# A recurrent attention with an MLP behind it: whole 128-token tiles for the first four units, 64x64 tiles for the rest

## The chip, the cores and the metric

The kernel runs on one core of a Trainium2 chip. The metric is the time of one execution on the device, in microseconds (us). The engines are TensorE (PE in the profile, with its weight loads as PEld), VectorE (DVE), ScalarE (ACT), GpSimd (POOL) and SyncE (SP), which issues the DMAs. Each engine takes its instructions in order and waits for others on semaphores.

## The reference

```python
# r, k, v, w: (batch 4, heads 8, tokens 768, 48); u: (8, 48)
state = 0                                            # (4, 8, 48, 48)
for t in range(768):
    y[t]  = r[t] @ (state + (u * k[t]) outer v[t])
    state = w[t][:, None] * state + k[t] outer v[t]
x = y as (3072, 384)                                 # tokens by heads*48
h = x @ w_in                                         # (384, 2048)
g = where(h > 0, h, exp(min(h, 0)) - 1)
out = g @ w_out                                      # (2048, 384)
```

The decay w lies between 0.80 and 0.95. All inputs are float32.

## The kernel before

The 768 tokens are six chunks (c = 0 to 5) of 128 tokens by 4 batches, 512 columns of x each. The attention of a chunk is done in four *units* of 128 rows, 24 units in all. A unit is a *pair*: 64 tokens of two batches, so units 0 and 1 of a chunk hold its first 64 tokens (batches 0, 1 and 2, 3), units 2 and 3 its other 64. The 8 heads lie as 4 pairs of heads (`NP`), one in partitions 0 to 47, one in 64 to 111.

A unit's steps, with the planner's names: `es` and `gs` are two scans on VectorE that turn w into running products inside the 64 tokens; `rh` and `kh` multiply r and k by them; `rkc`, `pd`, `md` and `sp` form the diagonal (u times r times k) and spread it over a matrix `am` (on ScalarE for units 0 to 7, on GpSimd later); `s` (`score`) transposes k and multiplies k with r; `mk` copies the scores above the diagonal into `am`; `v` (`value`) multiplies `am` with v, and k transposed with v (the update of the state, `pu`); `state_part`, half in `score`, half in `value`, adds r times the state. `xh` and `xl` take the result out of PSUM as two rounded parts; `sc` and `up` scale the state and add the update. Units 0 and 1 have no state before them (`first`): they skip `sc` and `state_part`, and ScalarE copies their update.

All of these matmuls are float32 in pieces of the array. Scores, state parts and values use tiles of 64 rows by 32 columns (`job`, and the loop over `j in range(4)` in `score` and `value`), the transposes and the diagonal the whole width. On the chip each such matmul of the code shows as two records; a transpose shows as one.

The MLP of a chunk has 16 steps (`f`), each with `g1` (9 matmuls, x times w_in), four small steps on ScalarE and VectorE (`r1`, `r2`, `stt`, `gh`, `gl`), and `g2` (9 matmuls into `acc`). Its operands are float32r, split into a high and a low part. In chunks 0 and 1 the first six steps are done in two halves of 256 columns (`FH`): the first needs only the chunk's units 0 and 1. The weights come in as 64-bit floats; for each f, ScalarE and VectorE convert them during chunk 0 (`a`, `cand`, `cb`, `cc`, `wh`, `wl`).

The order is made by `Plan.order`: it plays all steps through with the costs in `COST`, the buffer counts in `SLOTS` and the due times that follow from `BEGINS`, and lets each engine take, of what is ready, the step that is due first. The code is then emitted in that order; each engine runs its own list. SP issues the loads of w, k (with r), rk, v and of the raw weights from one queue in this order, and waits in it for buffers to come free.

Of the kernel before, what the change touches and what calls it, by code (L numbers as in the profile page):

```python
# [40 lines left out]
def _pieces():  # L41
    res = []
    for h in range(H):
        s, e = h * D, (h + 1) * D
        while s < e:
# [10 lines left out]
COST = dict(es=1.2, gs=1.5, pc=0.2, pd=0.9, md=0.2, spa=2.0, rh=0.62, kh=0.62, rk=0.48, rku=0.48, prk=1.2, prku=1.35, dg=0.5, mk=0.65, up=0.48, sc=0.48, xl=0.48,  # L56
            cand=0.56, cv=0.96, wl=0.88, stt=0.62, gl=0.64, fl=1.35, kt=0.53, xh=0.48, a=0.92, wh=0.82, r1=0.6, r2=0.62, gh=0.62,
            sp=1.95, s=1.4, s0=1.1, s2=0.95, v=1.4, v0=1.2, v2=0.95, g=2.05, out=0.6)
# [8 lines left out]
COLS = 128  # L67
PAD = 160
# [4 lines left out]
SLOTS = dict(w=2, k=3, rk=2, v=4, eg=2, md=2, am=2, kt=2, pa=1, pb=1, wg=2, ph=2, m=2, gh=2, gl=2, x=2, acc=1, raw0=1, x0=1, x1=1, x1a=1, x1b=1)  # L73
# [134 lines left out]
def mlp(nc, w_h, w_l, ps_acc, ps_h, ml, gp, po, dst, last=False):  # L208
# [9 lines left out]

    def g1(s, x):
        f, lo, hi = s["f"], s["lo"], s["hi"]  # L220
        xh, xl = (z[:, :, lo:hi] for z in x)
        s["ph"] = ph = ps_h.tile([P, N], F32, tag="ph", name="ph")[:, 0:hi - lo]
        for k in range(NK):
            for n, (w, x_) in enumerate(((w_h, xh), (w_h, xl), (w_l, xh))):
                for z in range(0, P, COLS):
                    nc.tensor.matmul(ph[z:z + COLS], w[:, f, 0, k, z:z + COLS], x_[:, k, :],  # L226
                                     start=(k == n == 0), stop=(k == NK - 1 and n == 2))
# [19 lines left out]
    def g2(s):  # L247
        f, lo, hi = s["f"], s["lo"], s["hi"]
        for m in range(NK):
            parts = 2 if (f == NF - 1 and m == NK - 1 and last) else 1  # L250
            for q in range(parts):
                s_ = slice(q * (hi - lo) // parts, (q + 1) * (hi - lo) // parts)
                a_ = accs()[m][:, lo + s_.start:lo + s_.stop]
                for n, (w, g) in enumerate(((w_h, s["gh"]), (w_h, s["gl"]), (w_l, s["gh"]))):
                    for z in range(0, P, COLS):
                        nc.tensor.matmul(a_[z:z + COLS], w[:, f, 1, m, z:z + COLS], g[:, s_],  # L256
                                         start=(f == n == 0 and lo == 0), stop=(f == NF - 1 and q == parts - 1 and n == 2))
# [22 lines left out]
def rwkv_elu_kernel(ctx, tc, wkr, rk, vp, u, uz, gkrw, gv, gu, wraw, out):  # L280
# [28 lines left out]
    upper = kp.tile([P, L], F32, name="upper")  # L309
    upper4 = upper.bitcast(U32).unsqueeze(1).unsqueeze(1).broadcast_to([P, 2, NP, L])  # L310
# [4 lines left out]
    units = [dict(c=i // B, b=(2 * (i % STEP), 2 * (i % STEP) + 1), i=i, first=i < STEP, last=i >= NU - STEP) for i in range(NU)]  # L315
    spans = lambda x: x.rearrange("d (s t) -> d s t", s=NS)
    scan = lambda x, z: spans(x[:, z])
    raws, xts = {}, {}

    def constants():  # L320
        nc.scalar.preload_act_table_set("natural_log_exp_and_others")
        nc.vector.memset(reset, 2.0 ** -62)
        nc.vector.memset(scan(reset, 0)[:, :, L:L + 1], 1.0)
# [3 lines left out]
        nc.vector.memset(upper, 1.0)  # L327
        for z in range(2):
            rs = slice(L * z, L * z + L)
            nc.gpsimd.affine_select(out=ident_h[rs], in_=ident_h[rs], pattern=[[1, L]], compare_op=ALU.is_equal,  # L330
                                    fill=0.0, base=0, channel_multiplier=-1)
            nc.gpsimd.affine_select(out=upper[rs], in_=upper[rs], pattern=[[1, L]], compare_op=ALU.is_gt,
                                    fill=0.0, base=0, channel_multiplier=-1)
# [47 lines left out]

    def r_hat(u_):
        r = spans(u_["r"].rearrange("d p t -> d (p t)"))
        tt(r, r, scan(u_["eg"], 1)[:, :, 0:L], ALU.mult)  # L384

    def k_hat(u_):
        k = spans(u_["k"].rearrange("d p t -> d (p t)"))
        tt(k, k, scan(u_["eg"], 0)[:, :, 1:L + 1], ALU.mult)

    def flag(u_):  # L390
        junk = at.tile([R2, 2, CWS], BF16, tag="junk", name="junk", bufs=1)
        act(junk, u_["eg"], AF.Relu, bias=lim, accum_out=flags[:, u_["i"]:u_["i"] + 1])  # L392
# [25 lines left out]
    def spread_act(u_):  # L418
        u_["am"] = am = at.tile([P, 2, NP, L], F32, tag="am", name="am", bufs=SLOTS["am"])
        for q in range(2):  # L420
            for p in range(NP):
                act(am[:, q, p], ident_h, AF.Copy, scale=u_["md"][:, q, p:p + 1])  # L422
# [14 lines left out]
    def state_part(u_, swap):  # L437
        for n in range(2 * NP):
            for h in range(2):
                p, x = HEADS[h ^ swap][n]  # L440
                rs, e = slice(64 * (x // 2), 64 * (x // 2) + D), (16, 48, 0, 32)[x]
                job(u_, h, p, x, st[rs, u_["b"][h], p, e:e + 32], u_["r"][rs, p, L * h:L * h + L], start=(swap == 1 and n < 4), stop=False)

    def score(u_):
# [5 lines left out]
        u_["pa"] = pa = both[:, :, 0:NP * L].rearrange("t q (p s) -> t q p s", p=NP)  # L450
        u_["pu"] = both[0:R2, :, 0:NP * D].rearrange("d h (p e) -> d h p e", p=NP)
        u_["py"] = both[:, :, NP * L:NP * L + NK * L].rearrange("d h (k t) -> d h k t", k=NK)
        for p in range(NP):
            for j in range(4):
                js, ts = slice(32 * j, 32 * j + 32), slice(64 * (j // 2), 64 * (j // 2) + L)
                for q in range(2):
                    rs = slice(64 * q, 64 * q + D)
                    nc.tensor.matmul(pa[js, 1 - q, p], u_["k"][rs, p, js], u_["r"][rs, p, ts], start=True, stop=True)  # L458
        if not u_["first"]:
            state_part(u_, 1)  # L460

    def mask(u_):
        nc.vector.copy_predicated(u_["am"], upper4, u_["pa"])
# [5 lines left out]
    def scale_state(u_):  # L469
        b = slice(u_["b"][0], u_["b"][0] + 2)  # L470
        tt(sv[:, b], sv[:, b], u_["pc"].rearrange("d (p h) o -> d h p o", h=2).broadcast_to([R2, 2, NP, D]), ALU.mult)

    def value(u_):
        v, am, kt = u_["v"], u_["am"], u_.get("kt")
        rows = [slice(L * h, L * h + L) for h in range(2)]
        if not u_["first"]:
            state_part(u_, 0)
        for n, (p, x) in enumerate(VALUES):
            for h, rs in enumerate(rows):
                job(u_, h, p, x, v[rs, P * p + 32 * x:P * p + 32 * x + 32], am[rs, 1 - x // 2, p],  # L480
                    start=(u_["first"] and n < 4), stop=(u_["last"] and n >= len(VALUES) - 4))
        if u_["last"]:
            return
        for p in range(NP):
            for j in range(4):
                js = slice(32 * j, min(32 * j + 32, R2))
                for h, rs in enumerate(rows):
                    nc.tensor.matmul(u_["pu"][js, h, p], kt[rs, p, js], v[rs, P * p + 80 * (j // 2):P * p + 80 * (j // 2) + D],  # L488
                                     start=False, stop=(p == NP - 1))

    def columns(u_, t):
        lo = u_["i"] % B * C
        return t[:, :, lo:lo + C].rearrange("d k (h t) -> d h k t", h=2)

    def x_high(u_):
# [3 lines left out]
        nc.scalar.copy(columns(u_, xts[c][0]), u_["py"])  # L499

    def x_low(u_):
        xh, xl = (columns(u_, t) for t in xts[u_["c"]])
        tt(xl, u_["py"], xh.bitcast(F32), ALU.subtract)  # L503

    def update(u_):
        b = slice(u_["b"][0], u_["b"][0] + 2)
        if not u_["first"]:
# [54 lines left out]
    for u_ in units:  # L562
# [6 lines left out]
        add(("es", i), "DVE", K["es"], lambda u_=u_: e_scan(u_), [("const",), ("ld_w", i)], lock=True)  # L569
# [3 lines left out]
        if not u_["first"]:  # L573
# [19 lines left out]
        if not u_["first"]:  # L593
            add(("sc", i), "DVE", K["sc"], lambda u_=u_: scale_state(u_), [("pc", i), ("up", i - STEP)], lock=True)
# [209 lines left out]
```

## Time and profile before

| | |
|---|---|
| runs | 557.33, 560.1, 564.27 us (median 560.1) |
| profiled execution | 559.8 us, span 558.0 us |
| granted TensorE clock, mean | 0.942 |
| PE busy | 515.2 us (92%), 8009 records |
| DVE, ACT, POOL busy | 348.4 us, 284.1 us, 69.9 us |
| data moved | 47.91 MB, mean 86 GB/s |

"Busy" counts the time in which an engine runs at least one instruction; small matmuls overlap, so their own durations add up to more. A row of a group or of a timeline gives the line, engine and operation, the tile written and the tiles read, and in brackets how long the engine stood idle before it and what ended that; "issue" is idle time for which the profile shows no releaser. The instruction queue (q8) carries the program itself to the engines.

### The profile page before, as it was taken

To read this page: it belongs to the slowest core of one execution; us is meant where nothing else is said; L and a number is where in the kernel's file an instruction comes from. 1 tells how busy PE (TensorE), PEld (TensorE's weight loads), DVE (VectorE), ACT (ScalarE), POOL (GpSimd) and SP (SyncE) were. 2 spreads that over 40 slices of the span, in tenths; PEclk is the share of its full clock that TensorE was granted. 3 is DMA by queue.
4 is the path that set the end of the run, shared out by engine and by line. 5 is a ranking of instruction groups with operands and counts; after the bars stand their busy time and mean duration, and the time that the engine had idled before them with its cause. 6 is when DMAs were issued, how large, how long until landed. Compare 5 with 4: busy or idle time off the path is not lost.

```text
span 558.0 us, 17756 instructions
## 1 busy us (share of the span) xinstructions
PE 515.2 (92%) x8009; PEld 433.9 (78%) x8009; DVE 348.4 (62%) x524; ACT 284.1 (51%) x564; POOL 69.9 (13%) x75
## 2 busy tenths in 40 slices
PE   6478789998889999999999999999999999999993
PEld 6368788886778887888888888888887888788882
DVE  7489789997546786249684358883377763333331
ACT  5367378776535445266443455553464544544441
POOL 1000000000111513003430003530032110000000
PEclk8556899998798999999999999999999999999998
DMA  8833945111532331014420055231052000010001
GB/s 263 254 117 121 288 140 170 56 35 59 179 97 75 110 93 57 4 53 142 115 64 2 2 167 152 80 98 55 2 173 80 3 3 1 12 47 1 0 0 62
DMA packets 17298, 47.91 MB, mean 86 GB/s; under 512 B 2112, under 2 KB 2496, under 8 KB 17216
## 3 DMA queue, kind: packets, MB, share of 16 engines
q1 hardware_dynamic: 17072, 46.57, 27.2%
q8 instruction: 65, 1.06, 0.8%
q14 instruction: 17, 0.14, 0.1%
q10 hardware_dynamic: 144, 0.13, 0.1%
HBM read 41.98 MB, written 4.72 MB: 84 GB/s over the span
## 4 chain that ended last, share of the span: by engine, by line
PE 86%; DVE 5%; issue 4%; ACT 3%; DMA 1%; DVEq 0%; ACTq 0%
PE acc L256 36%; PE ph L226 35%; PE pa L435 6%; PE pa L458 3%; PE pa L488 3%; PE pb L448 2%; PE pb L412 1%; ACT am L422 1%; DVE w_l L542 1%; DVE wg L532 1%; DMA w<-in_wkr_dram 1%; DVE wg L536 0%; DVE k L384 0%; DVE eg L379 0%; ACT wg L524 0%
## 5 line engine op out<-in xcount | busy, mean ns | idle before, releaser
L237 DVE SCALAR_TENSOR_TENSOR m<-m,ph 128x512 f32<-128x512 f32 (+1 forms) x108 | 67.4, 625 | 112.9 <-ACT m L234 112.3
L231 ACT ACTIVATE m<-ph 128x512 f32<-128x512 f32 (+1 forms) x108 | 59.2, 548 | 139.2 <-PE ph L226 138.6
L226 PE MATMUL ph<-xh,w_h 128*128 128x512 f32 (+1 forms) x324 | 124.6, 384 | 5.0 <-ACT w_h L539 1.7
L256 PE MATMUL acc<-gh,w_h 128*128 128x512 f32 (+1 forms) x325 | 124.5, 383 | 0.7 <-ACT gh L241 0.7
L226 PE MATMUL ph<-xh,w_l 128*128 128x512 f32 (+1 forms) x324 | 122.5, 378 | 2.4 <-DVE w_l L542 2.0
L256 PE MATMUL acc<-gl,w_h 128*128 128x512 f32 (+1 forms) x325 | 121.0, 372 | 1.8 <-issue 1.5
L226 PE MATMUL ph<-xl,w_h 128*128 128x512 f32 (+1 forms) x324 | 122.2, 377 | 0.2 <-DVE xl L503 0.2
L256 PE MATMUL acc<-gh,w_l 128*128 128x512 f32 (+1 forms) x325 | 121.2, 373 | 0.0
L245 DVE TENSOR_TENSOR gl<-m,gh 128x512 fp32r<-128x512 f32 (+1 forms) x108 | 69.0, 642 | 32.7 <-ACT gh L241 31.9
L241 ACT CAST gh<-m 128x512 fp32r<-128x512 f32 (+1 forms) x108 | 61.3, 571 | 45.0 <-DVE m L237 37.3
L226 PEld LDWEIGHTS ph<-xh,w_h 128*128 128x128 f32 x324 | 64.6, 199 | 16.7 <-ACT w_h L539 2.1
L226 PEld LDWEIGHTS ph<-xh,w_l 128*128 128x128 f32 x324 | 64.5, 199 | 13.5 <-DVE w_l L542 2.9
L256 PEld LDWEIGHTS acc<-gh,w_h 128*128 128x128 f32 x325 | 63.1, 194 | 12.8 <-ACT gh L241 1.1
L226 PEld LDWEIGHTS ph<-xl,w_h 128*128 128x128 f32 x324 | 64.7, 200 | 10.2 <-DVE xl L503 0.7
L256 PEld LDWEIGHTS acc<-gl,w_h 128*128 128x128 f32 x325 | 63.2, 195 | 12.0 <-issue 1.8
L256 PEld LDWEIGHTS acc<-gh,w_l 128*128 128x128 f32 x325 | 63.1, 194 | 10.3
L234 ACT ACTIVATE m<-m 128x512 f32<-128x512 f32 (+1 forms) x108 | 63.2, 585 | 3.3
L428 POOL TENSOR_SCALAR_AFFINE_SELECT am<-md 64x512 f32<-64x512 f32 x32 | 27.7, 864 | 220.4 <-DVE md L402 176.6
L395 POOL TENSOR_TENSOR rk<-rk 128x384 f32<-128x384 f32 x16 | 18.7, 1170 | 155.2 <-DMA rk<-in_rk_dram 154.8
L392 ACT ACTIVATE junk<-eg,lim 112x1040 bf16<-112x1040 f32 x24 | 27.8, 1158 | 11.0 <-DVE eg L379 11.0
L379 DVE TENSOR_TENSOR_SCAN eg<-w,reset 112x520 f32<-112x520 f32 x24 | 31.3, 1303 | 0.8
L370 DVE TENSOR_TENSOR_SCAN eg<-w,reset 112x520 f32<-112x520 f32 x24 | 30.5, 1269 | 1.6 <-DMA w<-in_wkr_dram 1.5
(73 smaller groups left out, 500.1 us busy)
## 6 DMA issues: line engine op xcount, KB each, us to landing
k<-in_wkr_dram SPq DMA_DIRECT2D x24, 448.0 KB, 4.8
wrawx<-in_wraw_dram SPq DMA_DIRECT2D x10, 768.0 KB, 4.5
v<-in_vp_dram SPq DMA_DIRECT2D x24, 256.0 KB, 5.9
rk<-in_rk_dram SPq DMA_DIRECT2D x16, 384.0 KB, 4.2
w<-in_wkr_dram SPq DMA_DIRECT2D x24, 227.9 KB, 3.9
wraw<-in_wraw_dram SPq DMA_DIRECT2D x6, 768.0 KB, 5.3
out_dram<-o SPq DMA_DIRECT2D x17, 256.0 KB, 2.3
ub<-in_u_dram SPq DMA_DIRECT2D x1, 192.0 KB, 9.9
```

Of the source, the lines that this page charges most:

```text
L226: nc.tensor.matmul(ph[z:z + COLS], w[:, f, 0, k, z:z + COLS], x_[:, k, :], start=(k == n == 0), stop=(k == NK - 1 and n == 2))
L231: act(s["m"], s["ph"], AF.Relu, scale=-1.0)
L234: act(s["m"], s["m"], AF.Exp, scale=-1.0)
L237: stt_(s["m"], s["m"], -1.0, s["ph"], ALU.add, ALU.max)
L241: nc.scalar.copy(s["gh"], s["m"])
L245: nc.vector.tensor_tensor(s["gl"], s["m"], s["gh"].bitcast(F32), ALU.subtract)
L256: nc.tensor.matmul(a_[z:z + COLS], w[:, f, 1, m, z:z + COLS], g[:, s_], start=(f == n == 0 and lo == 0), stop=(f == NF - 1 and q == parts ...
L370: nc.vector.tensor_tensor_scan(out=eg[:, 0][:, ::-1], data0=u_["w"][:, 1:CWS + 1][:, ::-1], data1=reset[:, 0][:, ::-1], initial=0.0, op0=A ...
L379: nc.vector.tensor_tensor_scan(out=u_["eg"][:, 1], data0=u_["w"][:, 0:CWS], data1=reset[:, 1], initial=0.0, op0=ALU.mult, op1=ALU.max)
L392: act(junk, u_["eg"], AF.Relu, bias=lim, accum_out=flags[:, u_["i"]:u_["i"] + 1])
L428: nc.gpsimd.affine_select(out=am[rs].rearrange("t q p s -> t (q p) s"), in_=u_["md"][rs].rearrange("t q p -> t (q p)").unsqueeze(2).broadc ...
L435: nc.tensor.matmul(u_["py"][32 * j:32 * j + 32, h, k], l, r, **flags)
```

## The change

Units 0 to 3 are now one batch by 128 tokens each (`whole`); the 20 others stay pairs. For a whole unit scores are 8 matmuls of the code with 128x128 outputs, values 16 with 32 output rows and 128 columns, the update 8. The scans run over 128 tokens; their constants (`reset`) are rewritten on GpSimd ahead of unit 4. None of the four has a state before it, so none has `sc` or `state_part`, and ScalarE copies each update. The mask and the diagonal of a whole unit are 128x128 per head. In the pairs, scores and updates go by 64x64 tiles: 16 matmuls each in place of 32. The columns of chunk 0's x keep their place; its half steps read and write them through a two-part view (`cut`, `fold`). There are three v buffers in place of four, and some costs of the planner changed. What is fed in is laid out to match.

```diff
-            sp=1.95, s=1.4, s0=1.1, s2=0.95, v=1.4, v0=1.2, v2=0.95, g=2.05, out=0.6)
+            sp=1.95, s=1.55, s0=1.6, s2=1.05, v=1.7, v0=1.55, v2=1.2, g=2.05, out=0.6)
-SLOTS = dict(w=2, k=3, rk=2, v=4, eg=2, md=2, am=2, kt=2, pa=1, pb=1, wg=2, ph=2, m=2, gh=2, gl=2, x=2, acc=1, raw0=1, x0=1, x1=1, x1a=1, x1b=1)
+SLOTS = dict(w=2, k=3, rk=2, v=3, eg=2, md=2, am=2, kt=2, pa=1, pb=1, wg=2, ph=2, m=2, gh=2, gl=2, x=2, acc=1, raw0=1, x0=1, x1=1, x1a=1, x1b=1)
...
+    units = [dict(c=i // B, i=i, whole=i < B, last=i >= NU - STEP, L=C if i < B else L,
+                  b=slice(i, i + 1) if i < B else slice(2 * (i % STEP), 2 * (i % STEP) + 2)) for i in range(NU)]
...
     def spread_act(u_):
-                act(am[:, q, p], ident_h, AF.Copy, scale=u_["md"][:, q, p:p + 1])
+                act(am[:, q, p], ident if u_["whole"] else ident_h, AF.Copy, scale=u_["md"][:, q, p:p + 1])
...
     def score(u_):
         for p in range(NP):
-            for j in range(4):
-                js, ts = slice(32 * j, 32 * j + 32), slice(64 * (j // 2), 64 * (j // 2) + L)
+            for lo in range(0, C, u_["L"]):
                 for q in range(2):
-                    rs = slice(64 * q, 64 * q + D)
-                    nc.tensor.matmul(pa[js, 1 - q, p], u_["k"][rs, p, js], u_["r"][rs, p, ts], start=True, stop=True)
+                    rs, ts = slice(64 * q, 64 * q + D), slice(lo, lo + u_["L"])
+                    nc.tensor.matmul(pa[ts, 1 - q, p], u_["k"][rs, p, ts], u_["r"][rs, p, ts], start=True, stop=True)
...
     def value(u_):
-        rows = [slice(L * h, L * h + L) for h in range(2)]
+        rows = [slice(0, C)] if whole else [slice(L * h, L * h + L) for h in range(2)]
...
         for p in range(NP):
-            for j in range(4):
-                js = slice(32 * j, min(32 * j + 32, R2))
-                for h, rs in enumerate(rows):
-                    nc.tensor.matmul(u_["pu"][js, h, p], kt[rs, p, js], v[rs, P * p + 80 * (j // 2):P * p + 80 * (j // 2) + D],
-                                     start=False, stop=(p == NP - 1))
+            for h, rs in enumerate(rows):
+                for z in range(2):
+                    m = 64 - 16 * z
+                    nc.tensor.matmul(u_["pu"][64 * z:64 * z + m, h, p], kt[rs, p, 64 * z:64 * z + m], v[rs, P * p + 80 * z:P * p + 80 * z + D],
+                                     start=whole, stop=(whole or p == NP - 1))
...
+        again = i > 0 and units[i - 1]["whole"] != u_["whole"]
+        if again:
+            add(("reset", i), "POOL", 1.2, lambda u_=u_: set_reset(nc.gpsimd, u_), [("gs", i - 1)])
```

Three places in the instruction order. A row has the line, the operation, the tile written and the tiles read, the shape of the output, and how many follow each other. First TensorE at the program's start, before: transposes and scores of units 0 and 1 (`pb`, then `pa` and `acc`), values and the first update matmuls of unit 0.

```order
L448 MATMUL pb<-ident,k 128x112 x4
L458 MATMUL pa<-k 32x64 x32
L448 MATMUL pb<-ident,k 128x112 x4
L458 MATMUL acc<-k 32x64 x32
L435 MATMUL pa<-am,v 32x64 x32
L488 MATMUL pa<-v,kt 32x48 x6
L488 MATMUL pa<-v,kt 16x48 x2
```

The same place now:

```order
L460 MATMUL pb<-ident,k 128x112 x4
L468 MATMUL pa<-k 128x128 x8
L460 MATMUL pb<-ident,k 128x112 x4
L468 MATMUL acc<-k 128x128 x8
L447 MATMUL pa<-am,v 32x128 x16
L503 MATMUL pa<-v,kt 64x48
L503 MATMUL pa<-v,kt 48x48
```

The order of the steps is the same; 32 scores became 8, 32 values 16, and an update of 32 (four times the last two rows) became one of 8. Unit 1's value follows, now behind the diagonal of unit 2.

Second, TensorE at the closing stretch of a pair unit inside the MLP, before: an MLP matmul, then the second half of the state part, the values and the first update matmuls.

```order
L256 MATMUL acc<-gh,w_l 128x512
L435 MATMUL pa<-k,st 32x64 x16
L435 MATMUL pa<-am,v 32x64 x32
L488 MATMUL pa<-v,kt 32x48 x6
L488 MATMUL pa<-v,kt 16x48 x2
```

And now:

```order
L260 MATMUL acc<-gh,w_l 128x512
L447 MATMUL pa<-k,st 32x64 x16
L447 MATMUL pa<-am,v 32x64 x32
L503 MATMUL pa<-v,kt 64x48
L503 MATMUL pa<-v,kt 48x48
```

State part and values are as they were; the update that ends the stretch is 16 matmuls (eight times the last two rows) in place of 32.

Third, ScalarE at the program's start, before, from the first unit's diagonal (`md`, `am`) to the first state copy; `wg` and `w_h` are steps of a weight conversion.

```order
L416 COPY md<-pb 128x8
L422 ACTIVATE am<-ident_h,md 128x64 x8
L416 COPY md<-pb 128x8
L524 ACTIVATE wg<-wraw 128x768
L422 ACTIVATE am<-ident_h,md 128x64 x8
L467 COPY kt<-pb 128x448
L392 ACTIVATE junk,flags<-eg,lim 112x1040
L467 COPY kt<-pb 128x448
L524 ACTIVATE wg<-wrawx 128x768
L499 CAST xh<-pa 128x2x3x64
L539 CAST w_h<-wg 128x768
L510 COPY st<-pa 112x8x48
```

And now:

```order
L428 COPY md<-pb 128x8
L434 ACTIVATE am<-ident,md 128x128 x8
L428 COPY md<-pb 128x8
L434 ACTIVATE am<-ident,md 128x128 x8
L544 ACTIVATE wg<-wraw 128x768
L482 COPY kt<-pb 128x448
L404 ACTIVATE junk,flags<-eg,lim 112x2x516
L544 ACTIVATE wg<-wrawx 128x768
L482 COPY kt<-pb 128x448
L559 CAST w_h<-wg 128x768
L519 CAST xh<-pa 128x6x64
```

The first conversion step (`wg<-wraw`) moved behind unit 1's diagonal, and both diagonals are of 128 columns.

More of the change, by code (lines that the diff above doesn't have):

```diff
@@ L308, in rwkv_elu_kernel @@
     ident_h = kp.tile([P, L], F32, name="ident_h")
-    upper = kp.tile([P, L], F32, name="upper")
-    upper4 = upper.bitcast(U32).unsqueeze(1).unsqueeze(1).broadcast_to([P, 2, NP, L])
+    upper = kp.tile([P, C], F32, name="upper")
+    upper_h = kp.tile([P, L], F32, name="upper_h")
+    above = {n: t.bitcast(U32).unsqueeze(1).unsqueeze(1).broadcast_to([P, 2, NP, n]) for n, t in ((C, upper), (L, upper_h))}
     ub = cst.tile([P, DM], F32, name="ub")
@@ L480, in value @@
                 job(u_, h, p, x, v[rs, P * p + 32 * x:P * p + 32 * x + 32], am[rs, 1 - x // 2, p],
-                    start=(u_["first"] and n < 4), stop=(u_["last"] and n >= len(VALUES) - 4))
+                    start=(whole and n < 4), stop=((whole or u_["last"]) and n >= len(VALUES) - 4))
         if u_["last"]:
@@ L592, in rwkv_elu_kernel @@
         before = []
[L593 to L594 removed]
+        if not u_["whole"]:
+            add(("sc", i), "DVE", K["sc"], lambda u_=u_: scale_state(u_), [("pc", i)] + [("up", x["i"]) for x in units[max(0, i - B):i - 1] if set(range(4)[x["b"]]) & set(range(4)[u_["b"]])], lock=True)
             before.append(("sc", i))
[L596 to L597 removed]
+        add(("s", i), "PE", K["s0" if u_["whole"] else "s2" if u_["last"] else "s"], lambda u_=u_: score(u_), [("rh", i), ("kh", i), ("sp", i), ("const",)] + before)
+        add(("mk", i), "DVE", K["mk0" if u_["whole"] else "mk"], lambda u_=u_: mask(u_), [("s", i), ("sp", i)])
         if not u_["last"]:
@@ L602, in rwkv_elu_kernel @@
             after.append(("v", i - 1))
-        add(("v", i), "PE", K["v0" if u_["first"] else "v2" if u_["last"] else "v"], lambda u_=u_: value(u_), after,
+        add(("v", i), "PE", K["v0" if u_["whole"] else "v2" if u_["last"] else "v"], lambda u_=u_: value(u_), after,
             due=BEGINS[c] - (B - 1 - i % B) * STAG - 2.0 if c > 1 else None)
@@ L607, in rwkv_elu_kernel @@
         if not u_["last"]:
-            add(("up", i), FIRST if u_["first"] else "DVE", K["up"], lambda u_=u_: update(u_), [("xl" if u_["first"] else "xh", i)])
+            add(("up", i), FIRST if u_["whole"] else "DVE", K["up"], lambda u_=u_: update(u_), [("xl" if u_["whole"] else "xh", i)])
     for f in range(NF):
```

129 lines of the change are left out of this document (73 added, 56 removed).

## The prediction

> **What bounds the kernel now.** I read the page first (busy time, the chain that ended last), then a table by stage, then what TensorE waited for.
>
> ```profile
> span 558.0 us, 17756 instructions
> PE 515.2 (92%) x8009; PEld 433.9 (78%) x8009; DVE 348.4 (62%) x524; ACT 284.1 (51%) x564; POOL 69.9 (13%) x75
> ...
> PE 86%; DVE 5%; issue 4%; ACT 3%; DMA 1%; DVEq 0%; ACTq 0%
> ```
>
> TensorE is busy for 92% of the span and is 86% of the chain; the third name, "issue", is time in which the engine waited for nothing that the profile shows. The stages, with columns PE, weight load, VectorE, ScalarE, GpSimd (busy us and instructions), granted clock, DMA share, GB/s:
>
> ```profile
> 0.00:29.00 29.00, 16.97 (x435) 15.23 (x436) 18.09 (x30) 12.49 (x31) 2.72 (x11) 0.65 0.82 249
> 29.00:53.00 24.00, 20.31 (x86) 18.56 (x86) 21.92 (x33) 17.72 (x45) 0.00 (x0) 0.50 0.40 132
> 53.00:75.00 22.00, 15.67 (x574) 13.90 (x573) 17.00 (x29) 11.03 (x21) 0.00 (x0) 0.92 0.79 236
> 75.00:126.00 51.00, 50.88 (x368) 44.09 (x366) 48.43 (x74) 38.99 (x79) 0.00 (x0) 1.00 0.28 90
> 126.00:173.00 47.00, 39.58 (x1097) 35.80 (x1098) 25.36 (x44) 21.80 (x62) 5.50 (x6) 0.85 0.40 117
> 173.00:558.00 385.00, 371.75 (x5457) 306.27 (x5455) 217.56 (x318) 182.10 (x330) 61.67 (x58) 1.00 0.19 58
> ```
>
> Up to 75 us no engine is full, and VectorE, which converts the weights, is the busiest (57.0 of 75). From 75 to 126 TensorE has no gap. From 126 to 173 it loses 7.4 us to gaps and runs at a clock of 0.85. After that it loses 13 us in 385. So from 75 us on, whatever TensorE is spared comes off the end. Its waits from 75 us on (total, times, longest):
>
> ```profile
> PE pa L488 <- issue: 4.7, 3, 2.3
> PE pb L412 <- issue: 1.5, 1, 1.5
> PE acc L256 <- issue: 1.5, 1, 1.5
> PE ph L226 <- issue: 1.4, 2, 1.0
> ```
>
> That is 9.1 us without a visible cause, nearly all right behind small matmuls. The longest of all lies earlier. These are the DMA queues over the span (packets, MB, share), in 17.6 to 23.7 us, and in 23.7 to 26.3 us, and the matmul that ended that gap:
>
> ```profile
> q8 instruction: 65, 1.06, 0.8%
> ...
> q1 hardware_dynamic: 722, 1.88, 105.4%
> ...
> q8 instruction: 1, 0.02, 3.1%
> ...
> 26.31 0.47 PE L435 MATMUL acc<-am,v 64*32 64x64 f32 x16 [5.11 <-issue]
> ```
>
> Sixty-five packets of 16 KB feed 8009 matmuls and as many weight loads: one per some 123 pairs. While the data queue filled the DMA engines (105%) no such packet moved; one moved in the next 2.6 us, and TensorE went on. I read "issue" as waiting for its own program. A later gap gives the pace:
>
> ```profile
> 425.32 0.45 PE L435 MATMUL pa<-k,st 48*32 48x64 f32 x32
> ...
> 426.28 0.62 PE L488 MATMUL pa<-v,kt 64*32 64x48 f32 x42
> 427.87 0.34 PE L488 MATMUL pa<-v,kt 64*16 64x48 f32 x19 [0.97 <-issue]
> ```
>
> A stretch of state, value and update matmuls began at 425.32, had run off its 32 state, 64 value and 42 of its update records at 426.90 (some 140 of 160), and got more at 427.87, 2.55 us after it began.
>
> **The change part by part.** The sum is made against the profiled execution: 559.8 us (span 558.0), beside a median of 560.1 over runs from 557.33 to 564.27.
>
> *Program supply.* An f32 matmul of the code is two records here (32 state matmuls of the code in the two halves of a unit are 64). A pair unit ran 64 score, 64 state, 64 value and 64 update records; now scores and updates are 32 each. The closing stretch is 32+64+32 = 128. Behind it come MLP matmuls: nine between 263.38 and 265.65 in the rows below, 0.25 us each. In the 2.55 us that a packet took, the new stretch uses 128 records (about 1.6 us) and some four matmuls: 132, under the 140 that were at hand. So most of the 9.1 us goes; I take 7.5, ends 0 and 9. The Trainium skill, "Runtime: NRT & Kernel Launch", section "Instruction fetch mechanics", says the same of the 16 KiB blocks but calls the cost of crossing one mostly hidden; the 5.11 us row speaks against "hidden" for stretches as dense as these, and by that rule the 7.5 us would be 0.
>
> *Clock.* Two stretches around such a gap:
>
> ```profile
> 138.32:141.73 3.41, 2.45 (x145) 2.26 (x134) 3.19 (x6) 1.43 (x4) 0.00 (x0) 1.00 0.63 230
> ...
> 145.15:148.56 3.41, 3.41 (x18) 3.28 (x17) 0.42 (x1) 1.42 (x5) 1.76 (x2) 0.50 0.98 296
> ```
>
> After a stretch with TensorE busy for only 2.45 of 3.41 us, a full one ran at half clock and got 18 matmuls through. From 126 to 173 us the clock of 0.85 costs at most 0.15 x 47 = 7 us. Without the gaps I take back 4.5; ends -3 (the denser order loses a stretch elsewhere) and 7.
>
> *64x64 tiles.* One pair unit now, and the part of its scores at its head:
>
> ```profile
> 261.80 0.55 PE L448 MATMUL pb<-ident,k 112*128 112x112 f32 x4
> 262.28 0.81 PE L458 MATMUL pa<-k 48*32 48x64 f32 x61
> ...
> 262.94 0.51 PE L435 MATMUL pa<-k,st 48*32 48x64 f32 x30
> 263.38 0.50 PE L256 MATMUL acc<-gh,w_h 128*128 128x512 f32 x1
> ...
> 265.65 0.46 PE L435 MATMUL pa<-k,st 48*32 48x64 f32 x32
> ...
> 266.61 0.78 PE L488 MATMUL pa<-v,kt 64*32 64x48 f32 x61
> 267.32 0.50 PE L256 MATMUL acc<-gh,w_h 128*128 128x512 f32 x1
> ...
> 262.27:262.52 0.25, 0.24 (x32) 1.00 0.00 0
> ```
>
> 64 scores take 0.62 us (262.28 to about 262.90), 9.7 ns each; the first 32, already queued, start within 0.25 us, 7.8 ns each. A 64-wide record uses twice the array: 15.6 ns, 0.50 us for 32, a gain of 0.12. The 64 updates take 0.71 us with the change to the next shape, about 0.60 without; with 48 columns to move I take 0.42 for 32, a gain of 0.18. Against it stand two changes of shape that were not there (64x64 scores to 64x32 state parts; 64x32 values to 64x64 updates). A change costs what 30 state records show, 0.44 us to the MLP matmul where 30 x 9.7 ns are 0.29: about 0.12 us. The rule that speaks against this change is in the Trainium skill, "TensorEngine Tiling (Array Packing)", section "Tiling Modes": changing the tile shape, not just the tile, drains the engine; the 0.12 us agrees. Net 0.12 + 0.18 - 0.24 = 0.06 us, over 20 pair units 1.2; I take 1.5, and as ends 7.5 gained (no drain) and 19 lost (two tiles share the array instead of four: 31 ns, 64 x 0.031 + 0.24 - 1.22 = 1.0 us a unit).
>
> *The first four units.* Rows for what they need:
>
> ```profile
> DVE xl L503 <- ACT xh L499: 9.7, 3, 4.8
> DVE am L463 <- PE pa L435: 2.1, 1, 2.1
> ...
> 1.44 4.28 PE L348 MATMUL pb<-ident 128*128 128x128 f32 x20 [1.44 <-POOL ident masks.py:199]
> ...
> 12.26 2.01 ACT L422 ACTIVATE am<-ident_h,md 128x64 f32<-128x64 f32 x8
> ...
> 16.97 0.73 DVE L463 COPY_PREDICATED am<-upper,acc 128x512 f32<-128x512 uint32 x1
> ...
> 15.68:16.54 0.86, 0.86 (x63) 0.50 0.97 401
> ...
> 0.00:17.52 17.52, 12.28 (x221) 10.91 (x221) 14.32 (x24) 10.37 (x27) 2.72 (x11) 0.75 0.92 287
> 19.20 0.36 PE L435 MATMUL pa<-am,v 64*32 64x64 f32 x8 [1.68 <-issue]
> ...
> 1.10 0.93 DVE L322 MEMSET reset<- 112x1040 f32 x1 [1.10 <-PEq L791]
> v<-in_vp_dram SPq DMA_DIRECT2D x24, 256.0 KB, 5.9
> ```
>
> TensorE: a whole 128x128 record took 0.214 us at the start. Unit 0 or 1 then has 16 scores on two row halves (1.7 us), 32 values on four column quarters (1.7) and 16 updates (0.9): 4.3 us. Before, 63 scores took 0.86 us (15.68 to 16.54), so three times 64 records 2.6: 1.7 more each now. Units 2 and 3 lose their 64 state records, the wait for a state update, and both VectorE steps on the state (their update becomes a copy on ScalarE). The order has 180 records ahead of the first MLP matmul, where 435 ran in the first 29 us before; that is less than the 221 that ran off before the first gap at 17.52, so the 1.68 and 5.11 us gaps go: -6.8 + 3.4, about 3.4 us earlier. ScalarE: diagonals of 128 columns lengthen the 2.01 us by between 0 and 2.0 (twice the columns); I take 0.4. Both stand ahead of the first weight conversion now, which starts some 2.5 us later. VectorE: a mask of 1024 columns costs at most the 0.73 us again, four times, some 2.5 us; four state steps go that pass 384 columns each (0.5 each, by the mask's 0.73 for 512): about even. What VectorE, the busiest engine here, waited for TensorE and its copies up to 75 us was 9.7 + 2.1 = 11.8 us; the 9.7 was for values whose matmuls stood in the gaps. Of it I take 7 back (5 at the second unit's value, 2 at units 2 and 3), covered by both engines: TensorE also idled 6 us from 53 to 75. Ends 0 and 11. Two edits I cost at nothing. The scan constants are written again on GpSimd ahead of unit 4, which VectorE's scan then waits for, with the conversions behind it; it can start as soon as unit 3's scans are done, long before (uncovered: about the 0.93 us of that memset on VectorE). With three v buffers in place of four a v load waits on SP for the value three units back, with weight loads queued behind it early on; the k load next to it has three buffers and waits for the same value already (uncovered: its 5.9 us to landing, once).
>
> Sum: 7.5 + 4.5 + 1.5 + 7 = 20.5; 559.8 - 20.5 = 539.3, say 539.
>
> **The rivals.** *The gaps are not the program's supply*, or the packets are late for another reason (data traffic): then gaps and clock stay, and 1.5 plus some 4 of the early 7 remain: 554. Against it stands the pair of queue rows; for it, that data held the 5.11 us up. 0.09. (The Trainium skill's "Runtime: NRT & Kernel Launch", as cited above, stands on this side.) *Two tiles at a time*: 559.8 - 19 + 19 = 560. No row before has four 64x64 tiles; the eight of 64x32 at 7.8 ns speak against it. 0.05. *One at a time*, the slower side: four transposes take 0.48 us, 0.12 for 128 columns, 0.06 for 64; 64 x 0.06 + 0.24 - 1.22 = 2.9 us a unit, 57 in all, 559.8 - 19 + 57 = 598. It beats the other gains from 30 ns a record on, and costs 2% from 39. 0.04. *The early stage turns on ScalarE*: if the conversions never make up their late start (2.5 us and twice 0.4), the 7 becomes -3.3, and the sum 10: 550. 0.07. *That the tiles are not what is said* is ruled out by the instruction order, where the shapes stand.
>
> **How the numbers follow.** The forecast, 525 to 549, has 0.75. With all terms at their good ends (9, 7, 7.5 and 11) it would be 525; I put the low end there. Upwards, 554 takes in ScalarE and the supply rival and leaves out the two tile rivals and a little of the forecast's own. 2% (548.9 and 571.3 around 560.1) is about what a measurement of this kernel tells from no change: faster 0.77 (the forecast and 0.02 of ScalarE's), same 0.18 (0.09, 0.05 of ScalarE's and 0.04 of two at a time), slower 0.05 (the rest).
>
> **What would show it.** Right: "issue" at TensorE under 4 us in all; no wait over 2 us before the first MLP matmul; a clock over 0.9 in the stretch where chunk 1 begins; 32 scores of a pair in 0.45 to 0.55 us. Wrong: "issue" of 15 us or more, scores of a pair over 0.62 us, or VectorE idle for more than 12 us before chunk 0 is half done. The forecast fails if TensorE stops being the engine without gaps after 75 us: waits for masks or conversions of over 5 us there.

## The result, and the profile after

| | before | after |
|---|---|---|
| median, range | 559.77 us (557.33 to 564.27, 4 runs) | 536.21 us (534.9 to 537.37, 4 runs) |
| profiled execution, span | 559.8, 558.0 us | 535.8, 534.1 us |
| granted TensorE clock, mean | 0.942 | 0.983 |
| instructions, TensorE records | 17756, 8009 | 14037, 6153 |

The ratio is 0.957 (95% interval 0.9505 to 0.9635): 23.6 us less. The prediction was 539 us in a range from 525 to 554.

The page of the changed kernel: span, busy time, granted clock in 40 slices, instruction queue, and the engines' shares of the chain that ended last.

```profile
span 534.1 us, 14037 instructions
PE 505.3 (95%) x6153; PEld 421.5 (79%) x6153; DVE 352.1 (66%) x521; ACT 284.6 (53%) x564; POOL 74.8 (14%) x78
PEclk9959999999999999999999999999999999999998
q8 instruction: 50, 0.82, 0.6%
PE 82%; DVE 9%; ACT 4%; issue 2%; DMA 1%; SPq 0%; DVEq 0%; ACTq 0%
```

TensorE's busy time fell by 9.9 us, and its time not busy from 42.8 to 28.8 us. "Issue" has half the share of the chain that it had, and the program takes 50 packets in place of 65. The stages of the changed kernel, in the columns of the prediction's table:

```profile
0.00:29.00 29.00, 22.13 (x194) 19.54 (x195) 23.20 (x35) 18.50 (x46) 2.96 (x12) 0.97 0.84 275
29.00:53.00 24.00, 18.46 (x151) 16.77 (x150) 23.79 (x38) 17.54 (x38) 1.08 (x2) 0.75 0.44 150
53.00:75.00 22.00, 19.19 (x194) 17.93 (x193) 21.14 (x36) 16.79 (x43) 0.00 (x0) 1.00 0.79 245
...
126.00:173.00 47.00, 44.97 (x843) 41.39 (x843) 34.22 (x57) 27.45 (x73) 13.92 (x14) 1.00 0.45 136
```

VectorE is busy for 68.1 of the first 75 us, where it was for 57.0: it does the same conversions with fewer holes. From 126 to 173 us, where chunk 1's units stand in the MLP, TensorE is busy for 5.4 us more and its clock is 1.00 in place of 0.85. What TensorE still waits for by "issue", over the whole span (total, times, longest):

```profile
PE pa L447 <- issue: 0.5, 1, 0.5
...
PE pa L503 <- issue: 0.4, 1, 0.4
```

Waits for "issue" are 0.9 us in all. Before, those after 75 us alone were 9.6: the four rows that the prediction adds up to 9.1, and this one, which its sum leaves out:

```profile
PE pa L435 <- issue: 0.5, 1, 0.5
```

To see where the time came from, I set the starts of the MLP's matmuls beside each other. Both kernels run the same ones in the same number, and with one exception the same units lie before each row below, so the n-th start tells how far the work has come. The exception is the 600th: by then the changed kernel has one closing stretch (1.7 us) less behind it.

| MLP matmul | before, us | after, us | gained |
|---|---|---|---|
| first | 29.2 | 25.7 | 3.5 |
| 100 | 65.7 | 56.5 | 9.1 |
| 300 | 104.7 | 95.4 | 9.3 |
| 400 | 144.8 | 127.4 | 17.4 |
| 600 | 187.2 | 163.4 | 23.9 |
| 1000 | 301.5 | 276.2 | 25.3 |
| last | 549.2 | 524.2 | 25.0 |

9.3 us come up to the 300th, before chunk 1, and 15.7 from there on. Of the 15.7 the table puts 14.6 between the 300th and the 600th, where chunk 1's units run; less the closing stretch still to come that is 12.9, and 2.8 come from all the rest.

### The profile page after: what moved, and what is told of

It is laid out like the page before. It is cut to its first block, busy times and chain, and to the rows that moved or that the text cites. A ratio compares the mean times of both kernels' runs of the same rounds, so it can differ in the third digit from the quotient of the medians.

```text
span 534.1 us, 14037 instructions
## 1 busy us (share of the span) xinstructions
PE 505.3 (95%) x6153; PEld 421.5 (79%) x6153; DVE 352.1 (66%) x521; ACT 284.6 (53%) x564; POOL 74.8 (14%) x78
## 4 chain that ended last, share of the span: by engine, by line
PE 82%; DVE 9%; ACT 4%; issue 2%; DMA 1%; SPq 0%; DVEq 0%; ACTq 0%
PE acc L260 35%; PE ph L232 34%; PE pa L447 6%; PE pa L468 2%; PE pa L503 2%; ACT am L434 2%; PE pb L460 1%; DVE wg L552 1%; DVE w_l L562 1%; DMA ubd<-in_uz_dram 1%; DVE m L242 1%; DVE gl L250 1%; DVE wg L556 1%; DVE eg L391 1%; PE pb L424 1%
## 5 line engine op out<-in xcount | busy, mean ns | idle before, releaser
L232 PE MATMUL ph<-xh,w_h 128*128 128x512 f32 (+1 forms) x324 | 122.0, 376 | 5.8 <-DVE m L242 2.5
L232 PE MATMUL ph<-xh,w_l 128*128 128x512 f32 (+1 forms) x324 | 120.2, 371 | 1.1 <-DVE w_l L562 1.1
L232 PE MATMUL ph<-xl,w_h 128*128 128x512 f32 (+1 forms) x324 | 120.1, 371 | 0.8 <-DVE xl L523 0.8
L260 PE MATMUL acc<-gh,w_l 128*128 128x512 f32 (+1 forms) x325 | 119.3, 367 | 0.0
L232 PEld LDWEIGHTS ph<-xh,w_h 128*128 128x128 f32 x324 | 62.2, 192 | 17.1 <-DVE m L242 3.0
L232 PEld LDWEIGHTS ph<-xh,w_l 128*128 128x128 f32 x324 | 62.3, 192 | 11.8 <-DVE w_l L562 1.8
L232 PEld LDWEIGHTS ph<-xl,w_h 128*128 128x128 f32 x324 | 62.3, 192 | 10.7 <-DVE xl L523 1.2
L440 POOL TENSOR_SCALAR_AFFINE_SELECT am<-md 64x512 f32<-64x512 f32 x32 | 29.5, 921 | 211.3 <-DVE md L414 172.8
L404 ACT ACTIVATE junk<-eg,lim 112x1040 bf16<-112x1040 f32 (+1 forms) x24 | 27.9, 1161 | 12.6 <-DVE eg L391 12.6
L381 DVE TENSOR_TENSOR_SCAN eg<-w,reset 112x520 f32<-112x520 f32 (+1 forms) x24 | 32.6, 1359 | 1.4 <-DMA w<-in_wkr_dram 1.4
L391 DVE TENSOR_TENSOR_SCAN eg<-w,reset 112x520 f32<-112x520 f32 (+1 forms) x24 | 31.9, 1328 | 0.8
```

The source lines that it names most:

```text
L232: nc.tensor.matmul(ph, w[:, f, 0, k], x_[:, k], start=(k == n == 0), stop=(k == NK - 1 and n == 2))
L260: nc.tensor.matmul(a_, w[:, f, 1, m], fold(s, g[:, s_]), start=(f == n == 0 and lo == 0), stop=(f == NF - 1 and q == parts - 1 and n == 2))
L381: nc.vector.tensor_tensor_scan(out=eg[:, 0, 0:n][:, ::-1], data0=u_["w"][:, 1:n + 1][:, ::-1], data1=reset[:, 0, 0:n][:, ::-1], initial=0. ...
L391: nc.vector.tensor_tensor_scan(out=u_["eg"][:, 1, 0:n], data0=u_["w"][:, 0:n], data1=reset[:, 1, 0:n], initial=0.0, op0=ALU.mult, op1=ALU.max)
L404: act(junk[:, :, 0:u_["n"]], u_["eg"][:, :, 0:u_["n"]], AF.Relu, bias=lim, accum_out=flags[:, u_["i"]:u_["i"] + 1])
L440: nc.gpsimd.affine_select(out=am[rs].rearrange("t q p s -> t (q p) s"), in_=u_["md"][rs].rearrange("t q p -> t (q p)").unsqueeze(2).broadc ...
```

## The experiments

My theory: TensorE waits for its own program where too many small records stand close together, above all in the closing stretch, and its clock falls around those waits; the tiles gain by having fewer records, not by faster arithmetic, and the whole units gain at the start. The main rival: the waits come from data traffic or from something else that the number of records doesn't touch, and the gain is the early stage's.

**The tiles alone.** The kernel before, with 64x64 tiles for scores and updates in all 24 pair units, and nothing else changed:

```diff
-            for j in range(4):
-                js, ts = slice(32 * j, 32 * j + 32), slice(64 * (j // 2), 64 * (j // 2) + L)
+            for lo in range(0, C, L):
...
-                    nc.tensor.matmul(pa[js, 1 - q, p], u_["k"][rs, p, js], u_["r"][rs, p, ts], start=True, stop=True)
+                    nc.tensor.matmul(pa[ts, 1 - q, p], u_["k"][rs, p, ts], u_["r"][rs, p, ts], start=True, stop=True)
...
-            for j in range(4):
-                js = slice(32 * j, min(32 * j + 32, R2))
-                for h, rs in enumerate(rows):
-                    nc.tensor.matmul(u_["pu"][js, h, p], kt[rs, p, js], v[rs, P * p + 80 * (j // 2):P * p + 80 * (j // 2) + D],
+            for h, rs in enumerate(rows):
+                for z in range(2):
+                    m = 64 - 16 * z
+                    nc.tensor.matmul(u_["pu"][64 * z:64 * z + m, h, p], kt[rs, p, 64 * z:64 * z + m], v[rs, P * p + 80 * z:P * p + 80 * z + D],
```

> The kernel before with one part of the change: all 24 units stay pairs, scores and updates go by 64x64 tiles (the order of the steps, the costs and the buffers are those of before). Theory (TensorE waits for its own program where some 140 records run off faster than a packet of it comes): a closing stretch is 128 records, so issue waits after 75 us fall from 9.1 us to under 2, and the clock between 126 and 173 us rises from 0.85 to 0.95 or more; ahead of the first MLP matmul stand 308 records, over the 221 that are at hand, so an early wait of 2 to 6 us stays and the early stage gains at most 3 us. Time 543 us (538 to 549). Rival 1 (the gain lies in the first four units being whole): 556 or more. Rival 2 (data traffic makes the waits, not the number of records): issue waits as before, 555 or more.

Measured: 540.28 us (539.25 to 541.51) beside 561.79 for the kernel before in this round, ratio 0.962 (0.9546 to 0.9693), as expected. What TensorE waited for by "issue" in this kernel, whole span:

```profile
PE pa L435 <- issue: 2.5, 2, 2.1
PE acc L435 <- issue: 2.3, 1, 2.3
PE acc L256 <- issue: 2.3, 1, 2.3
PE pa L487 <- issue: 0.4, 1, 0.4
```

Of this only 0.8 us lies after 75 us, and from 126 to 173 us the granted clock is 1.00. By the MLP's matmuls this kernel had gained 2.7 us at the 300th and 18.2 at the last, so 15.5 from there on; the changed kernel gained 15.7 there. The whole gain after the early stage is the tiles', with no unit made whole.

**The whole units alone.** The changed kernel with the pairs' scores and updates back on 64x32 tiles (the edit above, undone for pairs).

> The changed kernel with the pairs' scores and updates back on 32-wide tiles (64 records each again), all else as changed. Theory: the early stage keeps its gain of 9 us, the closing stretches have 160 records again, so issue waits of 6 to 9 us come back after 75 us and the clock between 120 and 170 us falls under 0.95 again: 550 us (546 to 555). Rival 1 (whole units carry it all): 537. Rival 2 (traffic): 537, as the loads are those of the changed kernel.

Measured: 553.74 us (548.57 to 555.15), ratio 0.9835 (0.9747 to 0.9923), inside the range that I expected, with more waits than the 6 to 9 us. The waits by "issue", and the stage from 126 to 173 us, of this kernel:

```profile
PE pa L504 <- issue: 7.3, 4, 2.5
PE acc L260 <- issue: 3.2, 2, 2.2
PE pa L447 <- issue: 0.8, 1, 0.8
PE ph L232 <- issue: 0.5, 1, 0.5
```

```profile
126.00:173.00 47.00, 42.20 (x997) 39.55 (x996) 26.52 (x50) 24.30 (x67) 10.67 (x11) 0.89 0.38 114
```

All 11.8 us lie after 75 us; the early waits are gone, those at the pairs are back, and the lower clock with them (0.89). So the early gain belongs to the whole units (7.1 us at the 300th matmul), the later one to the tiles. Alone the two gave 21.5 and 8.1 us, together 23.6 (in another round, where the kernel before took 559.77 us). That is 6.0 less than their sum. The 2.7 us that the tiles gain early in the first kernel are probably not there to be had twice; the rest is not accounted for.

**More records, in the one place and in the other.** The changed kernel with 16 extra matmuls of two columns (32 records) in each of 18 pair units; their results are read by nothing. In the first kernel they stand behind the update, where the closing stretch ends; in the second between scores and state part, in the opening stretch. The program has the same length in both. The cut shows the first; in the second the call stands in `score`, and the records write to the other half of `both` (`1 - q`).

```diff
+    def idle_records(u_):
+        for n in range(16):
+            z, q = n // 2 % 2, n % 2
+            rs, ts = slice(64 * q, 64 * q + D), slice(64 * z, 64 * z + 64)
+            nc.tensor.matmul(u_["both"][ts, q, 496:498], u_["k"][rs, n // 4, ts], u_["r"][rs, n // 4, 0:2], start=True, stop=True)
...
     def value(u_):
...
+        if not whole:
+            idle_records(u_)
```

> The changed kernel with 32 more records at the end of each closing stretch of 18 pair units: 16 matmuls of 2 columns whose results nobody reads. 160 records in a stretch again. Their own cost is between 8 ns each (4.6 us in all) and 16 ns each (9 us). Theory: issue waits go up from 0.9 us to 5 or more; 549 us (544 to 556). Rival (traffic): issue waits stay near 1 us and only their own cost is added: 541 to 545.

> The same 32 records added to the opening stretch instead (behind the scores): 100 records there, as before, and 128 in the closing one. The program is as long as in the run with the records at the end. Theory: own cost alone (4.6 to 9 us), issue waits under 2.5 us: 543 us (540 to 546), so clearly under the other. Rival (the length of the program, not the density of a stretch): as the other, within 2 us.

Measured: behind the update 555.14 us (552.04 to 557.72), ratio 0.9872 (0.9785 to 0.9959), some 19 us over the changed kernel and 6 more than I expected; behind the scores 543.4 (541.58 to 545.13), ratio 0.9681 (0.9602 to 0.9759), as expected. First the two largest of the "issue" waits with the records behind the update, 8.0 us in all:

```profile
PE pa L460 <- issue: 5.7, 4, 2.3
PE ph L232 <- issue: 1.3, 2, 0.9
...
```

Then with the records behind the scores:

```profile
PE pa L511 <- issue: 0.4, 1, 0.4
PE pb L466 <- issue: 0.3, 1, 0.3
```

The records themselves cost the same in both. Behind the update a closing stretch lasts 2.14 us (start of the state part to the next MLP matmul) where the changed kernel's lasts 1.70: 18 x 0.44 = 7.9 us:

```profile
206.19 0.46 PE L447 MATMUL pa<-k,st 48*32 48x64 f32 x32
...
208.33 0.50 PE L260 MATMUL acc<-gh,w_h 128*128 128x512 f32 x1
```

Behind the scores the opening stretch lasts 1.91 us in place of 1.49: 18 x 0.42 = 7.6 us, which is the whole 7.2 us by which that kernel is slower than the changed one.

```profile
209.84 0.55 PE L466 MATMUL pb<-ident,k 112*128 112x112 f32 x4
210.32 0.69 PE L474 MATMUL pa<-k 48*64 48x64 f32 x32
210.84 0.59 PE L460 MATMUL pa<-k 48*64 48x2 f32 x32
211.36 0.46 PE L447 MATMUL pa<-k,st 48*32 48x64 f32 x32
211.75 0.50 PE L260 MATMUL acc<-gh,w_h 128*128 128x512 f32 x1
```

The medians of the two lie 12 us apart, their profiled executions 14.3. Of that 7.3 us are the waits (8.0 against 0.7). At most 5.1 are the clock: the first kernel has three stretches of 3.41 us at half clock between 75 us and the last MLP matmul, the second none. Each begins within 1.5 us of the end of a wait. This is the second of the three, in the columns of the prediction's table; its granted clock is 0.50:

```profile
254.84:258.26 3.42, 3.42 (x10) 2.65 (x9) 1.06 (x3) 1.23 (x2) 0.19 (x1) 0.50 0.64 193
```

Some 2 us more lie at the start of the profiled executions, on which more below. So the same 32 records in another place make the waits, at the same length of the program and with the same data moved. Kernels with closing stretches of 128 have 0.2 to 3.0 us of "issue" waits after 75 us, those with 160 have 6.8 to 11.8, with records that do nearly no work just as with updates.

The traces also show what these waits are for. The ten profiles hold 51 "issue" waits of TensorE over 0.35 us. Each of them ends 1.1 to 1.6 us after a packet of q8 has landed. And if TensorE's instructions (matmuls, weight loads and its sequencer's own) are numbered by their starts, those at which the waits end are, within each kernel, a multiple of 256 apart, give or take one. TensorE stops where the instructions of one packet end and goes on when the next is there. So the number in a row is no threshold for each row: with 160 records, 4 of the 18 closing stretches of the kernel with scores alone (below) hold such a wait, two more have one a few MLP matmuls later, and twelve run through. Where in the row a packet ends seems to count too: ahead of each of those four waits 250 instructions, nearly a whole packet, had run off in 1.4 to 1.5 us.

**Less data traffic at the start.** The kernel before, with the loads of units 2 and 3 and of u planned for 22 us or later, so that they stand behind others in SP's queue:

```diff
-    add(("ub",), "SP", DMA_ISSUE, lambda: load_u(False), size=196.0)
+    add(("ub",), "SP", DMA_ISSUE, lambda: load_u(False), start=22.0, size=196.0)
...
-        early = max(0.0, BEGINS[c] - LEAD) if c > 0 else 0.0
+        early = max(0.0, BEGINS[c] - LEAD) if c > 0 else 22.0 if i > 1 else 0.0
```

> The kernel before, with the loads of units 2 and 3 and of u planned for 22 us or later, so that less data moves while TensorE runs units 0 and 1. The number of records ahead of the first MLP matmul stays 436. Theory (a packet is late because many records run off, and the data queue stretches that wait): the early wait of 5.11 us falls to 1.5 to 3 us, the waits after 75 us stay (7 to 10 us): 554 to 561 us. Rival (the data queue alone): no early issue wait over 1 us.

Measured in one run: 554.0 us, beside 560.23 (559.76 to 563.42) for the kernel before. The place where before the 5.11 us wait stood:

```profile
18.00 0.96 PE L435 MATMUL acc<-am,v 64*32 64x64 f32 x48
21.88 0.47 PE L435 MATMUL acc<-am,v 64*32 64x64 f32 x16 [2.92 <-issue]
```

The queues inside that gap, from 18.96 to 21.88 us:

```profile
q1 hardware_dynamic: 68, 0.32, 46.0%
q8 instruction: 1, 0.02, 2.6%
```

The data queue has 46% in this gap, where it had 70% over the other (101% in the half of it before the packet started to move), and the wait is 2.92 us in place of 5.11; one packet of the program moved in it, as before. The wait stays, though, and so do others, over the whole span:

```profile
PE pa L435 <- issue: 4.1, 2, 3.3
PE pa L488 <- issue: 3.8, 2, 2.5
```

The longest, 3.33 us, ends at 64.79 us, and there the data queue has 82%. So traffic goes with longer waits; it is not needed for one. The waits after 75 us come to 6.8 us, just under the 7 to 10 that I expected, 3.8 of them at the updates of line 488; they were 9.6. And in the kernel with scores alone (below) this wait stands where one packet, of 16 KB and of q8, is all that any queue moved from 428.00 to 431.36 us:

```profile
431.36 0.27 PE L503 MATMUL pa<-v,kt 64*32 64x48 f32 x6 [1.78 <-issue]
...
DMA packets 1, 0.02 MB, mean 5 GB/s; under 512 B 0, under 2 KB 0, under 8 KB 0
```

The time of 554.0 is a single run of an order that moved in other places too, and I read no more from it than that.

**Which of the two tiles.** The changed kernel with one of them undone for the pairs: first updates by 64x64 and scores by 64x32 (96 records in the opening stretch behind its transposes, 128 in the closing one), then the other way round (64 and 160).

```diff
-            for lo in range(0, C, u_["L"]):
+            for lo in range(0, C, u_["L"] if u_["whole"] else 32):
                 for q in range(2):
-                    rs, ts = slice(64 * q, 64 * q + D), slice(lo, lo + u_["L"])
-                    nc.tensor.matmul(pa[ts, 1 - q, p], u_["k"][rs, p, ts], u_["r"][rs, p, ts], start=True, stop=True)
+                    js = slice(lo, lo + (C if u_["whole"] else 32))
+                    rs, ts = slice(64 * q, 64 * q + D), slice(lo // 64 * 64, lo // 64 * 64 + u_["L"])
+                    nc.tensor.matmul(pa[js, 1 - q, p], u_["k"][rs, p, js], u_["r"][rs, p, ts], start=True, stop=True)
```

> The changed kernel with the pairs' scores back on 32-wide tiles (64 records), the updates left on 64x64. Opening stretch 100 records, closing 128. Theory: only the closing stretch ever ran over the 140; issue waits stay under 2 us after 75 us, and one change of shape less per unit pays for the scores: 536 us (533 to 540). Rival (the records of both stretches count): 541 or more.

> The changed kernel with the pairs' updates back on 32-wide tiles, the scores left on 64x64. Closing stretch 160 records again. Theory: issue waits of 5 to 9 us after 75 us and a lower clock where they lie, as with both undone: 550 us (546 to 555). Rival (half the records, half the effect): 544.

Measured: updates alone 542.13 us (538.35 to 542.8), ratio 0.9653 (0.9609 to 0.9697), 6 us above what I expected; scores alone 551.0 (550.06 to 552.44), ratio 0.9838 (0.9812 to 0.9864), as expected. The waits by "issue" with updates alone:

```profile
PE pa L447 <- issue: 1.8, 1, 1.8
PE pa L504 <- issue: 0.7, 1, 0.7
PE acc L260 <- issue: 0.5, 1, 0.5
```

And the two largest with scores alone:

```profile
PE pa L503 <- issue: 8.4, 4, 3.0
PE ph L232 <- issue: 2.9, 2, 1.9
```

The closing stretch is where the program mostly runs out. My expectation that the scores' tiles are worth nothing beside it was wrong. With updates alone the "issue" waits are 3.0 us against 0.9; an opening stretch takes 1.58 us (from 255.66 to 257.24) against 1.49, which is 1.8 us over 20 units; and some 2 us are lost at the start of the profiled execution (7.3 us gained at the 300th MLP matmul against 9.3). These three make up the 6 us. So the scores' tiles are worth something too, if less than the updates'. The count of records alone doesn't explain the waits among the three: the kernel with idle records behind the scores has the same 96 and 128, and 0.7 us of waits. In records the two kernels answer to the two with idle records: 96 and 128 gave 542 here and 543 there, 64 and 160 gave 551 here and 555 there, whether the extra records compute something or not.

**The diagonal's place.** In the changed kernel the first MLP matmul waits for the copy of unit 1, which stands on ScalarE behind unit 2's diagonal. Rows of ScalarE and TensorE in the changed kernel:

```profile
22.63 2.45 ACT L434 ACTIVATE am<-ident,md 128x128 f32<-128x128 f32 x8
...
25.19 0.47 ACT L519 CAST xh<-acc 128x384 fp32r<-128x384 f32 x1
```

```profile
25.71 0.39 PE L232 MATMUL ph<-xh,w_h 128*128 128x256 f32 x1 [1.71 <-ACT xh L519]
```

One edit makes the diagonal follow the copy:

```diff
+        if i == 2:
+            plan.tasks[("sp", 2)]["after"].append(("xh", 1))
```

> The changed kernel with one more rule of order: ScalarE spreads unit 2's diagonal (2.45 us) only after it has taken unit 1's values out of PSUM. Theory: the first MLP matmul, which waited 1.7 us for that, starts 1.2 to 1.7 us earlier, but VectorE with the conversions is the limit of the early stage, so of it 0 to 1 us reaches the end: 535.5 us (534 to 537.5). Rival (TensorE is the limit there): 534.5 or less; rival (the diagonal is missed later): 537.5 or more.

Measured: 536.42 us (535.17 to 538.19), ratio 0.9567 (0.9533 to 0.9601): the changed kernel's own time, and no gain. The wait before the first MLP matmul fell from 1.71 to 0.58 us, but that matmul came no earlier (27.0 us in its profile, against 25.7, at a lower granted clock), and at the 300th the kernel had gained 6.7 us. And TensorE now waits for unit 2's diagonal itself, ahead of that unit's transposes, where the changed kernel waits 0.50 us:

```profile
44.64 0.98 PE L460 MATMUL pb<-ident,k 112*128 112x112 f32 x4 [3.53 <-ACT am L434]
```

The edit moved a wait rather than took it away. That is what the second rival describes, though the time stayed inside my range. It doesn't show what the 1.71 us would be worth if nothing came in its place.

This run also says how far the early 9.3 us can be trusted. The clock granted in the first 50 us differs between profiled executions of kernels that have the same first four units. This is the granted clock by slices in the last kernel; the changed kernel's is among the first lines of its page above.

```profile
PEclk8567999999999999999999999999999999999998
```

At the 300th MLP matmul the six other kernels whose first four units are whole had gained 6.2, 6.7, 7.1, 7.3, 8.2 and 8.2 us (7.3 on average) where the changed kernel's profile has 9.3. So some 2 us of that 9.3 go with a clock that was high in that one execution.

## Why the prediction was right

**Sum and sign.** 20.5 us forecast against 23.6 by the medians and 25.0 at the last MLP matmul of the two traces. Beside each other, by stage: early 7 against 9.3 (7.3 on average in the six other kernels); supply, clock and tiles together 13.5 against 15.7.

**Program supply (7.5).** Right, and slightly small: 9.6 us after 75 us (9.1 in the prediction's sum) became 0.9, so 8.7 came back. The count behind it, 132 records in the time of a packet against 140 at hand, is right in its direction: stretches of 128 leave little waiting, stretches of 160 much, whether the 32 more are updates (11.6 us with scores alone) or idle records (8.0). As a limit for one stretch it is not: the 140 were read off a single row, and a wait falls where a packet ends, so that 12 of 18 stretches of 160 ran through. The rival that the gaps are not the program's supply (554 us) falls: with no data moved otherwise and the same program length, the place of 32 records alone makes 7.3 us of waits. Its half-truth is the 5.11 us wait, which traffic seems to have stretched. The Trainium skill, "Runtime: NRT & Kernel Launch", section "Instruction fetch mechanics", calls the crossing of a block mostly hidden. Here it is hidden among large matmuls and in most dense stretches, and costs 8.4 us in four of the 18 stretches of 160 small records of the kernel with scores alone.

**Clock (4.5).** Right that it comes back with the waits, small in size. The stage from 126 to 173 us went from 0.85 to 1.00, and what is left of the gain for the clock is 25.0 - 9.3 - 8.7 - 1.2 = 5.8 us. The rows allow at most 6.8: between 75 us and the last MLP matmul the kernel before spends 13.65 us at half clock, the changed one nothing. The clock follows the waits: 0.89 with whole units alone, 0.93 with the late loads, 0.96 with scores alone or with idle records behind the update, 1.00 in every kernel whose "issue" waits after 75 us are 3 us or less. In the ten profiles there are 14 stretches at half clock between 75 us and the last MLP matmul; each begins within such a wait or at most 2.5 us after one. The reverse doesn't hold: the wait of 1.78 us shown above brought no such stretch. Why one wait does and another doesn't stays open.

**64x64 tiles (1.5).** Right as a sum, with its parts shifted. One unit of the changed kernel, its opening stretch from the transposes and its closing stretch from the state part to the next MLP matmul:

```profile
270.37 0.55 PE L460 MATMUL pb<-ident,k 112*128 112x112 f32 x4
270.85 0.69 PE L468 MATMUL pa<-k 48*64 48x64 f32 x32
271.47 0.46 PE L447 MATMUL pa<-k,st 48*32 48x64 f32 x32
271.86 0.50 PE L260 MATMUL acc<-gh,w_h 128*128 128x512 f32 x1
```

```profile
238.45 0.45 PE L447 MATMUL pa<-k,st 48*32 48x64 f32 x32
...
239.55 0.67 PE L503 MATMUL pa<-v,kt 64*64 64x48 f32 x32
240.15 0.50 PE L232 MATMUL ph<-xh,w_h 128*128 128x512 f32 x1
```

32 scores take 0.62 us up to the state part (270.85 to 271.47), and 0.52 where more records of their own shape follow (210.32 to 210.84 in the kernel with idle records there). So the scores are 0.52 and the change of shape 0.10, against 0.50 and 0.12. The opening stretch went from 1.58 to 1.49 us, where I had it even; the closing one from 1.67 to 1.70, where I had 0.06 gained: its 32 updates take 0.60 up to the MLP, so about 0.50 without the change, against 0.42. Net 0.06 us a unit, as forecast, and in part by luck: the prediction's price of a change was a slip, as 0.44 - 0.29 is 0.15 and not 0.12, and with 0.15 its net would have been about nothing. The two tile rivals, 1.0 and 2.9 us a unit slower, are out. The Trainium skill, "TensorEngine Tiling (Array Packing)", section "Tiling Modes", says that a change of the tiling mode drains TensorE. The trace agrees, with the 0.10 us of a change. That price uses up nearly all that the larger tiles save, and it is the number of records that gains.

**The first four units (7).** The first MLP matmul came 3.5 us earlier (3.4 forecast; that close by luck, since in the six other kernels it came 2.1 to 3.1 us earlier) and the diagonal of 128 columns took 2.45 us (2.4). VectorE's largest wait in the first 75 us, in the changed kernel, and the only one for values or scores:

```profile
DVE am L478 <- PE pa L468: 2.8, 1, 2.8
```

Of the 11.8 us for values and scores 2.8 are left in this execution, so 9.0 came back, of which I had taken 7. I took "5 at the second unit's value, 2 at units 2 and 3" from a stage that I then saw in one execution only; six others put it between 6.2 and 8.2 us. The rival by which ScalarE turns the early stage into a loss (550 us) is out: VectorE is busy for 68.1 of the 75 us, and all seven kernels with whole units had gained 6.2 to 9.3 us by the 300th MLP matmul.

**What would show it.** "Issue" under 4 us in all: 0.9. No wait over 2 us before the first MLP matmul: the longest is 1.71. A clock over 0.9 where chunk 1 begins: 1.00. 32 scores in 0.45 to 0.55 us: 0.52 among their own kind.

## What to carry to other kernels

Where TensorE waits behind a row of small matmuls and the profile shows no releaser, look whether a packet of the instruction queue landed just before TensorE went on, count the records in the row, and set them against the time that a packet takes. Fewer, larger tiles took most of these waits away here, though the arithmetic got hardly faster. Such waits can cost more than their own length, since the granted clock fell right behind many of them. Price a stage from more than one execution when its clock differs from one to the next. And before a visible wait is counted as a gain, look what would wait in its place: here 1.71 us came back as 3.53 elsewhere.

## What the runs showed of the hardware

A record with two columns was not cheap: 32 of them in the opening stretch cost 0.42 us, 13 ns each, where 32 scores of 64 columns on the same tiles took 0.52 us, 16 ns each. A stretch of such records is limited more by their number than by the columns they move.

Where the same 32 records stand was worth 12 us of 543, though the program was equally long. I had expected 6. The waits are 7.3 of the 14.3 us between the profiled executions, and the half clock behind them at most 5.1.

The clock granted in the first 29 us was 0.97 in the profiled execution of the changed kernel and lower in those of its near copies, while the medians with the diagonal moved and not moved are 536.42 and 536.21. What sets that early clock stays open.
